# Eight key transposes of one shape, scores in pairs, wider tie matmuls and a hand-written merge at the start of an attention-and-router kernel

## The chip, the cores and the metric

One core of a Trainium2 chip runs the whole kernel. The metric is device time in microseconds (us). Three runs of the kernel before gave 258.41, 258.51 and 258.77; the median is 258.51.

## The reference

```python
# q, k, v: 8 batches x 8 heads x 576 positions x 64
k_p = k.reshape(B, H, Sp, pool, D).mean(axis=3)      # pool = 8, Sp = 72
v_p = v.reshape(B, H, Sp, pool, D).mean(axis=3)
scores = scale * np.matmul(q, k_p.transpose(0, 1, 3, 2))
attn = softmax(scores)
x = (attn @ v_p)            # to 4608 rows x 512
xn = x / (norm(x) + 1e-6);  en = emb / (norm(emb) + 1e-6)
logits = xn @ en.T / tau    # 8 experts
idx = argmax(logits)        # one expert per row
gate_w = softmax(logits)[row, idx]
out[row] = gate_w * (relu(x[row] @ w1[idx]) @ w2[idx])
...
```

Every row goes to one expert. The kernel works on one batch (576 rows) at a time with the expert that most of its rows chose; a loop behind it, empty for these inputs, would handle rows of a batch that chose another.

## The kernel before

The kernel has two kinds of work per batch, and writes their instructions out in one order by hand (a manual schedule): every engine then runs its own instructions in that order. TensorE is written PE in the profile, VectorE DVE, ScalarE ACT, GpSimd POOL, SyncE SP.

The attention side of a batch is a list of steps with costs (`attn_steps`, line 130). `pool_kv` pools keys and values with 18 matmuls of 64-row weights (`pool_mm`, line 140); ScalarE copies the pooled keys to memory in `kp_out` (line 152), VectorE the values in `vp_out`. `qtr` transposes queries, nine per group of four heads (line 191). `kpt` (line 196) transposes the pooled keys of four head pairs into one PSUM tile: per pair one transpose of 128 columns and two of 64 columns with the halves swapped, so that each head's keys exist on partitions 0 to 63 and on 64 to 127. `score` (line 220) makes one head's scores with two matmuls on 64 rows each, and ScalarE takes the exponential (line 237). `pv` (line 241) multiplies by the values for 128 rows, all heads, and VectorE normalises (lines 257, 259). `xtr` (line 264) transposes the result; VectorE copies it (line 275), ScalarE squares it (line 281). `route` (line 284) makes the logits and `count` (line 306) counts the rows per expert; each of the two starts with a matmul of one row that adds a tiny penalty to break ties (lines 287, 307). `expert` (line 313) takes the largest count, and GpSimd reads it into a register and issues the loads of that expert's weights, then of the inputs two batches ahead.

The FFN side (`ffn_steps`, line 422) has eight groups `hgrp` of eight matmuls (line 434), then eight half blocks `yblk` of four matmuls (line 452) and one last step. Results are scaled by the gate and stored on SP's queue.

PSUM has four tiles of two banks, which every one of these steps takes in turn. Weights have three buffers, inputs three, output tiles four.

The order is a merge by due times. Each attention step of batch b has the due time b plus its share of the batch's cost; before an FFN step at position p, all attention steps with due times under p + 1.7 (`LEAD`) are written out. Batch 0's attention is written first as a whole up to its first 128 rows and its expert; the rest of it (its tail) is put among batch 1's steps by due times between 1.0 and 1.4. In batch 0's scores there are extra matmuls on a tile of ones (`fill`, line 214) whose results nobody reads.

Of the kernel before, what the change touches and what calls it, by code (L numbers as in the profile page):

```python
# [11 lines left out]
FP16 = mybir.dt.float16  # L12
# [15 lines left out]
def kernel(  # L28
# [84 lines left out]
    ident_h = const.tile([128, 128], FP16)  # L113
    pmat = const.tile([128, T, G], FP16)
    ones_m = const.tile([128, 512], FP16)
    tie_l = const.tile([1, NC * E], FP16)
    tie_n = const.tile([1, E], FP16)
    half_c = const.tile([128, NC], FP32)
    lnxs = const.tile([128, 1], FP32)
    enT = const.tile([128, 4, E], FP16)  # L120
# [4 lines left out]
    icol = const.tile([128, 1], FP32)  # L125
    pair_b = const.tile([1, B * E], I32)
    pair_e = const.tile([1, B * E], I32)


    def attn_steps(b):  # L130
# [20 lines left out]

        def kp_out(src, h0, nh):

            kp = att.tile([G, nh, 2, D], FP16, name=f"kp{nh}")
            nc.scalar.copy(out=kp, in_=src)
            for hp in range(nh):
                st['kp', h0 + hp] = kp[:, hp]

        def vp_out(src):
            vpx = att.tile([G, HP, 2, D + 1], FP16, name="vpx")  # L160
# [35 lines left out]
        def kpt(h0, nh):  # L196


            pk = psum().bitcast(FP16)
            for hp in range(nh):  # L200
                src = st['kp', h0 + hp]
                nc.tensor.transpose(out=pk[:, ts(2 * hp, G)],
                                    in_=src.rearrange("g r d -> g (r d)"),
                                    identity=ident_h[:G, :G])
                for r in range(2):
                    nc.tensor.transpose(out=pk[ts(r, 64), ts(2 * hp + 1, G)],
                                        in_=src[:, 1 - r], identity=ident_h[:G, :G])
            kpT = att.tile([128, 2 * nh, G], FP16, name=f"kpT{nh}")
            nc.vector.tensor_copy(
                out=kpT, in_=pk[:, 0:2 * nh * G].rearrange("p (h g) -> p h g", g=G))  # L210
            for i in range(2 * nh):
                st['kpT', 2 * h0 + i] = kpT[:, i]

        def fill(cols, n):

            for _ in range(n):
                nc.tensor.matmul(out=cols, lhsT=ones_m[:, 0:128],
                                 rhs=ones_m[:, 0:cols.shape[-1]], start=True, stop=True)

        def score(h, nfill=0):  # L220
            grp, sub, h2 = h // 4, (h // 2) % 2, h % 2
            qT = st['qT', grp]
            pS = psum()
            fill(pS[:, 0:192], nfill)

            for even in (True, False):
                half = sub if even else 1 - sub
                rows = ts(half, 64)
                c0, nb = (512 - 320, 5) if even else (512, 4)
                blk = ds(5 * sub if not even else 4 * sub, nb)  # L230
                nc.tensor.matmul(  # L231
                    out=pS[0:G, c0:c0 + nb * 64].rearrange("g (t p) -> g t p", p=64),
                    lhsT=st['kpT', h if half == 0 else h ^ 1][rows, :],
                    rhs=qT[rows, blk, ts(h2, 64)],
                    start=True, stop=True)
            at = atp.tile([G, S], FP16, name="at")
            nc.scalar.activation(out=at, in_=pS[0:G, 512 - 320:512 + 256], func=AF.Exp,  # L237
                                 scale=escale)
            st['at', h] = at
# [21 lines left out]
                in1=r.unsqueeze(2).to_broadcast([128, H, D]), op=ALU.mult)  # L261
            st['xs'][c] = x_sb

        def xtr(c):
            L = 128 if c < 4 else 64
            x_sb = st['xs'][c]
            xf = x_sb.rearrange("p h d -> p (h d)")
            pt = psum().bitcast(FP16)
            for w in range(4):
                nc.tensor.transpose(out=pt[:, w * 128:w * 128 + L],  # L270
                                    in_=xf[0:L, ts(w, 128)],
                                    identity=ident_h[:L, :L])
            ptv = pt[:, 0:512].rearrange("p (w t) -> p w t", t=128)
            if c < 4:
                nc.vector.tensor_copy(out=xt_all[:, b, :, ts(c, 128)], in_=ptv)  # L275
            else:
                nc.vector.tensor_copy(
                    out=xt_all[:, b, :, ts(c, 128)].rearrange("p w (r t) -> p w r t", r=2),
                    in_=ptv[:, :, 0:L].unsqueeze(2).to_broadcast([128, 4, 2, L]))
            sq = xp.tile([128, H * D], FP16, name="sq", bufs=1)  # L280
            nc.scalar.activation(out=sq, in_=xf, func=AF.Square,  # L281
                                 accum_out=st['ssq'][:, c:c + 1])

        def route(c0, n):

            pl = psum()
            nc.tensor.matmul(out=pl[:, 0:n * E], lhsT=ones_m[0:1, 0:128],
                             rhs=tie_l[:, 0:n * E], start=True, stop=False)
            for c in range(n):
                for w in range(4):  # L290
                    nc.tensor.matmul(out=pl[:, ts(c, E)],
                                     lhsT=xt_all[:, b, w, ts(c0 + c, 128)],
                                     rhs=enT[:, w, :],
                                     start=False, stop=(c == n - 1 and w == 3))
            plv = pl[:, 0:n * E].rearrange("p (c e) -> p c e", e=E)
            if 'lg' not in st:
                st['lg'] = rt.tile([128, NC, E], FP32, name="lg")
                st['lmax'] = rt.tile([128, NC], FP32, name="lmax")
            cs = ds(c0, n)
            lmax = st['lmax'][:, cs]  # L300
            bc = lmax.unsqueeze(2).to_broadcast([128, n, E])
            nc.vector.tensor_reduce(out=lmax, in_=plv, axis=AX.X, op=ALU.max)
            nc.vector.tensor_tensor(out=oh_all[:, b, cs], in0=plv, in1=bc, op=ALU.is_ge)
            nc.vector.tensor_tensor(out=st['lg'][:, cs], in0=plv, in1=bc, op=ALU.subtract)

        def count(cs, pc):
            nc.tensor.matmul(out=pc[:, 0:E], lhsT=ones_m[0:1, 0:128], rhs=tie_n,
                             start=True, stop=False)
            for c in cs:
                nc.tensor.matmul(out=pc[:, 0:E], lhsT=ones_m[:, 0:128],  # L310
                                 rhs=oh_all[:, b, c], start=False, stop=(c == cs[-1]))

        def expert(cs):

            pc = psum()
            count(cs, pc)
            mx = rt.tile([128, E], FP32, name="mx")
            nc.vector.max(out=mx, in_=pc[:, 0:E])
# [26 lines left out]
        if b == 0:  # L345
            for grp in range(2):
# [3 lines left out]
                for h in range(4 * grp, 4 * grp + 4):  # L350
                    step(0.65)(lambda h=h: score(h, (12, 4, 4, 4, 10, 4, 4, 4)[h]))
                    if h == 5:
                        step(1.0)(pool_v)
            step(0.3)(emb_transposed)
            P(0)
            X(0)
            step(0.4)(lambda: route(0, 1))
            step(0.4)(lambda: expert([0]))
            step(0.0)(lambda: load_qkv(2))
            head, steps = steps, []  # L360
            for c in range(1, NC):
                P(c)
                X(c)
            step(0.8)(lambda: route(1, 4))
            step(0.4)(recount)
            return head, steps
# [1 line left out]
        step(0.8)(lambda: qtr(0))  # L368
        step(0.5)(lambda: kpt(0, HP))
        step(0.8)(lambda: qtr(1))  # L370
        for h in range(8):
            step(0.65)(lambda h=h: score(h))
        P(0)
        P(1)
        X(0)
# [132 lines left out]
        return finish  # L508


    def emb_transposed():
        pe = psum().bitcast(FP16)
        for w in range(4):
            nc.tensor.transpose(out=pe[:, ts(w, E)], in_=emb_h[:, ts(w, 128)],
                                identity=ident_h[:E, :E])
        nc.vector.tensor_copy(out=enT, in_=pe[:, 0:4 * E].rearrange("p (w e) -> p w e", e=E))

    with tc.manual_schedule():
# [18 lines left out]
        for i in range(9):  # L537
# [13 lines left out]
                                op=ALU.is_equal)  # L551
        nc.vector.tensor_scalar(out=ident_h, in0=irow, scalar1=icol, scalar2=None,
                                op0=ALU.is_equal)
        nc.vector.tensor_scalar(out=tie_n, in0=irow[0:1, 0:E], scalar1=-2.0 ** -10,
                                scalar2=None, op0=ALU.mult)
        nc.vector.tensor_scalar(
            out=tie_l.rearrange("p (c e) -> p c e", e=E),
            in0=irow[0:1, 0:E].unsqueeze(1).to_broadcast([1, NC, E]),
            scalar1=-2.0 ** -14, scalar2=None, op0=ALU.mult)

# [11 lines left out]
        head, tail = attn_steps(0)  # L572
        for _, f in head:
            f()
        astream = []
        for i, (_, f) in enumerate(tail):
            astream.append((1.0 + 0.4 * i / len(tail), f))
        for b in range(B):
            if b:
                steps = attn_steps(b)  # L580
                total = sum(c for c, _ in steps)
                done = 0.0
                for c, f in steps:
                    astream.append((b + done / total, f))
                    done += c
            for i, f in enumerate(gate_steps(b)):
                astream.append((b + LEAD + 0.05 + 0.12 * i, f))
        astream.sort(key=lambda s: s[0])
        j = 0
        for b in range(B):  # L590
            steps = ffn_steps(lambda b=b: xt_all[:, b], lambda b=b: weights[b],
# [1 line left out]
            total = sum(c for c, _ in steps)  # L593
            done = 0.0
            for c, f in steps:
                while j < len(astream) and astream[j][0] < b + done / total + LEAD:
                    astream[j][1]()
                    j += 1
                f()
# [80 lines left out]
```

## Time and profile before

| what | value |
|---|---|
| median of three runs | 258.51 us |
| the profiled execution | 257.43 us |
| its span, first to last instruction | 255.8 us |
| TensorE busy | 90% |
| TensorE weight loads (overlap) | 56% |
| VectorE, ScalarE, GpSimd busy | 51%, 42%, 17% |
| mean granted TensorE clock | 0.954 of full |
| DMA, software queue; hardware queue | 70.1%; 12.5% of 16 engines |

The busy time of TensorE counts a matmul from its first column to its modelled end, and neighbours overlap, so distances from start to start say more than durations. The granted clock is 1.00 at 2.4 GHz and 0.50 at 1.2 GHz. A DMA share can be over 1, since packets on one engine overlap.

### The profile page before, as it was taken

The page shows a single profiled execution, that of the slowest core. Times are in us where ns is not written, and L with a number is a line of the kernel's source. Part 1 is how long each engine was busy: PE and PEld are TensorE (multiplying, and loading weights), DVE is VectorE, ACT ScalarE, POOL GpSimd, SP SyncE. Part 2 cuts the span into 40 slices and gives each one's busy share as a digit, 9 for nine tenths or more (in the row PEclk, how much of TensorE's full clock was granted, in tenths as well). Part 3 has the DMA queues.
Part 4 walks back from the last instruction along what each step waited for, and adds up shares of the span by engine and source line. Part 5 has one row for each costly group of instructions (what it writes and reads, how often), then busy time and mean ns, then how long its engine had stood idle before and what let it go on. Part 6 is the DMA issues. An engine that isn't in the chain of part 4 may idle for free. (4 is left out here: it accounts for less than half of the span.)

```text
span 255.8 us, 5655 instructions
## 1 busy us (share of the span) xinstructions
PE 230.0 (90%) x2272; PEld 143.2 (56%) x2273; DVE 129.5 (51%) x368; ACT 108.1 (42%) x221; POOL 42.9 (17%) x61
## 2 busy tenths in 40 slices
PE   7796788999989998999899998999899999996950
PEld 3574555764566546673676456654666377564520
DVE  3225564862576428661685257642876178414310
ACT  3342364524463355417362446335541746124120
POOL 7300510060003400070006100340004000400000
PEclk9998755999999999999999999999999999999995
DMA  5994899249993999589994999299968952597061
GB/s 76 194 208 81 145 209 208 50 75 210 212 257 51 202 200 247 140 139 211 230 215 65 213 209 258 53 204 201 243 146 135 209 118 55 93 208 215 3 145 46
DMA packets 27597, 40.79 MB, mean 159 GB/s; under 512 B 1960, under 2 KB 15272, under 8 KB 27568
## 3 DMA queue, kind: packets, MB, share of 16 engines
q0 software_dynamic: 21152, 30.94, 70.1%
q1 hardware_dynamic: 6416, 9.46, 12.5%
q8 instruction: 19, 0.31, 0.5%
q14 instruction: 10, 0.08, 0.1%
HBM read 61.88 MB, written 9.44 MB: 279 GB/s over the span
## 5 line engine op out<-in xcount | busy, mean ns | idle before, releaser
L434 PE MATMUL pa<-xt_all,w 128*128 128x288 f16 x512 | 71.9, 288 | 2.4 <-ACT y_sb L482 2.4
L452 PE MATMUL pa<-w,hT 128*128 128x512 f16 x256 | 63.7, 380 | 0.0
L434 PEld LDWEIGHTS <-w 128*128 128x128 f16 x512 | 47.3, 99 | 16.5 <-issue 5.0
L237 ACT ACTIVATE at<-pa 72x576 f16<-72x576 f32 x64 | 38.2, 642 | 34.1 <-PE pa L231 33.9
L452 PEld LDWEIGHTS <-hT 128*128 128x128 f16 x256 | 21.5, 97 | 23.9 <-issue 2.8
L93 POOL DMA_DIRECT2D w<-in_moe_w_dram x8 | 6.3, 791 | 169.8 <-DVE vpx L161 145.7
L441 ACT ACTIVATE hT<-pa 128x576 f16<-128x576 f32 x32 | 20.7, 650 | 29.3 <-PE pa L434 29.1
L464 DVE TENSOR_SCALAR y_sb<-pa,gm 128x512 f32<-128x512 f32 x16 | 12.0, 751 | 34.9 <-PE pa L452 34.9
L259 DVE TENSOR_TENSOR x_sb<-pa,r 128x512 f16<-128x512 f32 x40 | 27.7, 691 | 2.6
L281 ACT ACTIVATE sq<-x_sb 128x512 f16<-128x512 f16 x40 | 25.0, 625 | 7.1 <-DVE x_sb L259 6.7
L443 DVE TENSOR_SCALAR hT<-pa 128x576 f16<-128x576 f32 x32 | 24.1, 753 | 5.5 <-PE pa L434 5.3
L462 ACT ACTIVATE y_sb<-pa,gm 128x512 f32<-128x512 f32 x16 | 11.0, 687 | 37.2 <-DVE y_sb L464 37.2
L250 PE MATMUL pa<-vpx,at 72*128 72x65 f16 (+1 forms) x384 | 19.7, 201 | 2.7 <-ACT hT L441 1.1
L250 PEld LDWEIGHTS <-at 72*128 72x128 f16 (+1 forms) x384 | 16.5, 106 | 9.8 <-issue 3.7
L270 PE MATMUL pa<-ident_h,x_sb 128*128 128x128 f16 (+1 forms) x160 | 15.2, 223 | 6.8 <-DVE x_sb L259 3.8
L145 PE MATMUL pa<-kv,pmat 64*72 64x512 f16 (+2 forms) x180 | 19.5, 366 | 0.0
L231 PE MATMUL pa<-qT,kpT 64*72 64x256 f16 (+1 forms) x128 | 18.8, 320 | 0.5
L257 DVE RECIPROCAL r<-pa 128x8 f32<-128x8 f32 x40 | 8.1, 202 | 22.1 <-PE pa L250 22.0
L270 PEld LDWEIGHTS <-x_sb 128*128 128x128 f16 (+1 forms) x160 | 10.6, 100 | 13.0 <-issue 5.4
L193 DVE COPY qT<-pa 128x1152 f16<-128x1152 f16 x16 | 12.1, 757 | 11.1 <-PE pa L191 10.2
L231 PEld LDWEIGHTS <-kpT 64*72 64x72 f16 x128 | 6.5, 111 | 16.0 <-issue 13.3
L275 DVE COPY xt_all<-pa 128x512 f16<-128x512 f16 x32 | 13.3, 415 | 2.2 <-PE pa L270 2.0
(94 smaller groups left out, 202.8 us busy)
## 6 DMA issues: line engine op xcount, KB each, us to landing
w<-in_moe_w_dram POOLq DMA_DIRECT2D x16, 1024.0 KB, 10.5
out_dram<-y_sb SPq DMA_DIRECT2D x64, 128.0 KB, 6.2
kv<-in_v_dram POOLq DMA_DIRECT2D x8, 576.0 KB, 19.0
kv<-in_k_dram POOLq DMA_DIRECT2D x7, 576.0 KB, 15.2
qq<-in_q_dram POOLq DMA_DIRECT2D x7, 576.0 KB, 22.9
out_dram<-y_sb SPq DMA_DIRECT2D x16, 64.0 KB, 5.8
kv<-in_k_dram POOLq DMA_DIRECT2D x2, 288.0 KB, 5.3
qq<-in_q_dram POOLq DMA_DIRECT2D x2, 288.0 KB, 6.3
```

Of the source, the lines that this page charges most:

```text
L145: nc.tensor.matmul(out=pk[0:G, par * 512 + c0:par * 512 + c0 + na * nh * D], lhsT=pmat[rows, t, :], rhs=kv[rows, a0:a0 + na, h0:h0 + nh, t ...
L231: nc.tensor.matmul(out=pS[0:G, c0:c0 + nb * 64].rearrange("g (t p) -> g t p", p=64), lhsT=st['kpT', h if half == 0 else h ^ 1][rows, :], r ...
L237: nc.scalar.activation(out=at, in_=pS[0:G, 512 - 320:512 + 256], func=AF.Exp, scale=escale)
L250: nc.tensor.matmul(out=px[rows, h * 128:h * 128 + D + 1], lhsT=st['at', h][:, c * 128:c * 128 + L], rhs=st['vpx'][:, h // 2, h % 2, :], st ...
L259: nc.vector.tensor_tensor(out=x_sb, in0=pxv[:, :, 0:D], in1=r.unsqueeze(2).to_broadcast([128, H, D]), op=ALU.mult)
L270: nc.tensor.transpose(out=pt[:, w * 128:w * 128 + L], in_=xf[0:L, ts(w, 128)], identity=ident_h[:L, :L])
L275: nc.vector.tensor_copy(out=xt_all[:, b, :, ts(c, 128)], in_=ptv)
L281: nc.scalar.activation(out=sq, in_=xf, func=AF.Square, accum_out=st['ssq'][:, c:c + 1])
L434: nc.tensor.matmul(out=ph[:, half * 512:half * 512 + HALF], lhsT=w1v[:, kk, w // 2, w % 2, :], rhs=xt()[:, kk, ts(half, HALF)], start=(kk ...
L441: nc.scalar.activation(out=dst, in_=src, func=AF.Relu)
L443: nc.vector.tensor_scalar(out=dst, in0=src, scalar1=0.0, scalar2=None, op0=ALU.max)
L452: nc.tensor.matmul(out=py, lhsT=st['hT'][:, w // 2, w % 2, ts(c, 128)], rhs=w2[:, w // 2, w % 2, :], start=(w == 0), stop=(w == 7))
```

## The change

Key transposes: the key tile gets nine heads' room for eight heads (2 x nh + 1), and a second ScalarE copy puts head 0 behind the last one. Eight transposes each take the 128 columns of two neighbouring heads, every next one 64 columns further; head i is then on partitions 0 to 63 of slot i and on 64 to 127 of slot i - 1.

Scores: batches 1 to 7 have steps of two heads with twice the cost.

Tie matmuls: the two penalty tiles get 128 rows, of which all but the first are zero, and the matmuls use all rows.

Start: fills are added ahead of the embedding transposes (8), and in batch 0's first transpose (14), route (8) and expert (12); batch 0's tail interleaves products and transposes, and 18 steps of it and of batch 1's first eight are written in a fixed order. The lead is 1.5 at the first FFN step and rises to 1.7 at the end of batch 0's FFN. The gate steps have a list of their own, sorted in with the rest.

```diff
-    tie_l = const.tile([1, NC * E], FP16)
-    tie_n = const.tile([1, E], FP16)
+    tie_l = const.tile([128, NC * E], FP16)
+    tie_n = const.tile([128, E], FP16)
...
-            kp = att.tile([G, nh, 2, D], FP16, name=f"kp{nh}")
-            nc.scalar.copy(out=kp, in_=src)
-            for hp in range(nh):
-                st['kp', h0 + hp] = kp[:, hp]
+            kp = att.tile([G, 2 * nh + 1, D], FP16, name=f"kp{nh}")
+            nc.scalar.copy(
+                out=kp[:, 0:2 * nh].rearrange("g (h r) d -> g h r d", r=2), in_=src)
+            nc.scalar.copy(out=kp[:, 2 * nh], in_=src[:, 0, 0])
+            st['kp', h0] = kp
...
-            for hp in range(nh):
-                src = st['kp', h0 + hp]
-                nc.tensor.transpose(out=pk[:, ts(2 * hp, G)],
-                                    in_=src.rearrange("g r d -> g (r d)"),
+            src = st['kp', h0].rearrange("g h d -> g (h d)")
+            for i in range(2 * nh):
+                nc.tensor.transpose(out=pk[:, ts(i, G)], in_=src[:, i * D:i * D + 128],
                                     identity=ident_h[:G, :G])
-                for r in range(2):
-                    nc.tensor.transpose(out=pk[ts(r, 64), ts(2 * hp + 1, G)],
-                                        in_=src[:, 1 - r], identity=ident_h[:G, :G])
...
-        def xtr(c):
+        def xtr(c, nfill=0):
...
-            pt = psum().bitcast(FP16)
+            pt = psum()
+            fill(pt[:, 512:704], nfill)
+            pt = pt.bitcast(FP16)
...
-            nc.tensor.matmul(out=pl[:, 0:n * E], lhsT=ones_m[0:1, 0:128],
+            fill(pl[:, 512:704], nfill)
+            nc.tensor.matmul(out=pl[:, 0:n * E], lhsT=ones_m[:, 0:128],
                              rhs=tie_l[:, 0:n * E], start=True, stop=False)
...
-            nc.tensor.matmul(out=pc[:, 0:E], lhsT=ones_m[0:1, 0:128], rhs=tie_n,
+            nc.tensor.matmul(out=pc[:, 0:E], lhsT=ones_m[:, 0:128], rhs=tie_n,
                              start=True, stop=False)
...
-            step(0.3)(emb_transposed)
+            step(0.3)(lambda: emb_transposed(8))
             P(0)
-            X(0)
-            step(0.4)(lambda: route(0, 1))
-            step(0.4)(lambda: expert([0]))
+            step(0.6)(lambda: xtr(0, 14))
+            step(0.4)(lambda: route(0, 1, 8))
+            step(0.4)(lambda: expert([0], 12))
...
-            for c in range(1, NC):
-                P(c)
-                X(c)
+            P(1)
+            P(2)
+            X(1)
+            P(3)
+            X(2)
+            P(4)
+            X(3)
+            X(4)
...
-        for h in range(8):
-            step(0.65)(lambda h=h: score(h))
+        for h in range(0, 8, 2):
+            step(1.3)(lambda h=h: [score(h), score(h + 1)])
...
+                for f in [s1[0], tail[0], s1[1], tail[1], tail[2], s1[2], s1[3], tail[3],
+                          tail[4], s1[4], tail[5], tail[6], s1[5], tail[7], s1[6], tail[8],
+                          s1[7], tail[9]]:
+                    f()
+                astream = astream[8:]
...
+        def lead(pos):
+            return pos + LEAD - 0.2 * max(0.0, 1.0 - pos)
...
-                while j < len(astream) and astream[j][0] < b + done / total + LEAD:
+                while j < len(astream) and astream[j][0] < lead(b + done / total):
```

## Rows read from the trace of the kernel before

**Rows 1.** Busy time by stretch, one period of the steady state; columns in the first line.
```profile
core 0: us, PE busy (x) PEld busy (x) DVE busy (x) ACT busy (x) POOL busy (x), PEclk, DMA share, GB/s
...
79.10:106.70 27.60, 26.73 (x275) 16.54 (x273) 15.65 (x43) 13.12 (x28) 4.98 (x6) 1.00 0.96 185
```

**Rows 2.** Busy time by stretch, the start; columns as above.
```profile
19.40:23.10 3.70, 1.68 (x24) 1.20 (x23) 1.88 (x7) 1.47 (x4) 0.00 (x0) 1.00 0.75 129
...
24.00:27.00 3.00, 3.00 (x16) 1.09 (x12) 0.73 (x2) 0.00 (x0) 1.75 (x3) 0.50 0.06 8
...
28.00:30.00 2.00, 0.61 (x12) 0.44 (x8) 1.97 (x5) 0.64 (x3) 0.98 (x2) 1.00 1.09 197
...
31.00:44.00 13.00, 10.98 (x120) 7.44 (x120) 7.59 (x20) 7.51 (x16) 1.20 (x1) 0.50 1.16 209
```

**Rows 3.** Timeline of TensorE at the start: start us, us, engine, line, operation, count.
```profile
9.27 1.16 PE L217 MATMUL pa<-ones_m 128*128 128x192 f16 x12
...
23.48 3.69 PE L145 MATMUL pa<-kv,pmat 64*72 64x512 f16 x18
...
40.16 0.68 PE L250 MATMUL pa<-vpx,at 72*128 72x65 f16 x9 [0.30 <-ACT at L237]
...
42.81 1.91 PE L434 MATMUL pa<-xt_all,w 128*128 128x288 f16 x8
```

**Rows 4.** Timeline of TensorE, key transposes of a steady batch.
```profile
83.62 1.14 PE L434 MATMUL pa<-xt_all,w 128*128 128x288 f16 x8
84.60 0.20 PE L202 MATMUL pa<-ident_h,kp 72*128 72x72 f16 x1
84.73 0.22 PE L206 MATMUL pa<-ident_h,kp 72*64 72x72 f16 x2
...
85.76 0.68 PE L191 MATMUL pa<-ident_h,qq 128*128 128x128 f16 x9
```

**Rows 5.** Timeline of TensorE, scores and values products between FFN blocks.
```profile
87.23 0.46 PE L231 MATMUL pa<-qT,kpT 64*72 64x320 f16 x4
87.62 1.04 PE L452 MATMUL pa<-w,hT 128*128 128x512 f16 x4
88.59 0.32 PE L231 MATMUL pa<-qT,kpT 64*72 64x320 f16 x2
88.84 1.04 PE L452 MATMUL pa<-w,hT 128*128 128x512 f16 x4
...
92.37 0.71 PE L231 MATMUL pa<-qT,kpT 64*72 64x320 f16 x4
93.01 1.04 PE L452 MATMUL pa<-w,hT 128*128 128x512 f16 x4
...
94.43 1.03 PE L452 MATMUL pa<-w,hT 128*128 128x512 f16 x4
95.30 0.42 PE L250 MATMUL pa<-vpx,at 72*128 72x65 f16 x8
95.56 1.03 PE L452 MATMUL pa<-w,hT 128*128 128x512 f16 x4
```

**Rows 6.** Groups of ScalarE from 25 to 40 us: busy us, mean ns, idle before.
```profile
L237 ACT ACTIVATE at<-pa 72x576 f16<-72x576 f32 x8 | 4.7, 644 | 1.1 <-PE pa L231 1.1
L281 ACT ACTIVATE sq<-x_sb 128x512 f16<-128x512 f16 x4 | 2.5, 630 | 3.8 <-DVE x_sb L259 3.8
...
L155 ACT CAST kp<-pa 72x512 f16<-72x512 f32 x1 | 0.6, 581 | 5.0 <-PE pa L145 5.0
```

**Rows 7.** Timeline of TensorE, count with its tie matmul, and merged pooling.
```profile
77.69 1.14 PE L434 MATMUL pa<-xt_all,w 128*128 128x288 f16 x8
78.76 0.17 PE L307 MATMUL pa<-tie_n,ones_m 1*128 1x8 f16 x1
78.87 0.28 PE L310 MATMUL pa<-oh_all,ones_m 128*128 128x8 f16 x5
79.08 2.13 PE L145 MATMUL pa<-kv,pmat 64*72 64x512 f16 x18
```

More of the change, by code (lines that the diff above doesn't have):

```diff
@@ L127, with fill @@
     pair_e = const.tile([1, B * E], I32)
+    def fill(cols, n):
+        for _ in range(n):
+            nc.tensor.matmul(out=cols, lhsT=ones_m[:, 0:128],
+                             rhs=ones_m[:, 0:cols.shape[-1]], start=True, stop=True)
     def attn_steps(b):
@@ L211, in kpt @@
             for i in range(2 * nh):
[L212 to L218, printed above, removed]
+                st['kpT', 2 * h0 + i, 0] = kpT[0:64, i]
+                st['kpT', 2 * h0 + (i + 1) % (2 * nh), 1] = kpT[64:128, i]
         def score(h, nfill=0):
@@ L232, in score @@
                     out=pS[0:G, c0:c0 + nb * 64].rearrange("g (t p) -> g t p", p=64),
-                    lhsT=st['kpT', h if half == 0 else h ^ 1][rows, :],
+                    lhsT=st['kpT', h, half],
                     rhs=qT[rows, blk, ts(h2, 64)],
@@ L282, in xtr, with route @@
                                  accum_out=st['ssq'][:, c:c + 1])
-        def route(c0, n):
+        def route(c0, n, nfill=0):
             pl = psum()
-            nc.tensor.matmul(out=pl[:, 0:n * E], lhsT=ones_m[0:1, 0:128],
+            fill(pl[:, 512:704], nfill)
+            nc.tensor.matmul(out=pl[:, 0:n * E], lhsT=ones_m[:, 0:128],
                              rhs=tie_l[:, 0:n * E], start=True, stop=False)
@@ L311, in count, with expert @@
                                  rhs=oh_all[:, b, c], start=False, stop=(c == cs[-1]))
-        def expert(cs):
+        def expert(cs, nfill=0):
             pc = psum()
+            fill(pc[:, 512:704], nfill)
             count(cs, pc)
@@ L508, in store, with emb_transposed @@
         return finish
-    def emb_transposed():
-        pe = psum().bitcast(FP16)
+    def emb_transposed(nfill):
+        pe = psum()
+        fill(pe[:, 512:704], nfill)
+        pe = pe.bitcast(FP16)
         for w in range(4):
@@ L553 @@
                                 op0=ALU.is_equal)
-        nc.vector.tensor_scalar(out=tie_n, in0=irow[0:1, 0:E], scalar1=-2.0 ** -10,
+        nc.vector.memset(tie_n, 0.0)
+        nc.vector.memset(tie_l, 0.0)
+        nc.vector.tensor_scalar(out=tie_n[0:1], in0=irow[0:1, 0:E], scalar1=-2.0 ** -10,
                                 scalar2=None, op0=ALU.mult)
         nc.vector.tensor_scalar(
-            out=tie_l.rearrange("p (c e) -> p c e", e=E),
+            out=tie_l[0:1].rearrange("p (c e) -> p c e", e=E),
             in0=irow[0:1, 0:E].unsqueeze(1).to_broadcast([1, NC, E]),
@@ L574 @@
             f()
-        astream = []
-        for i, (_, f) in enumerate(tail):
-            astream.append((1.0 + 0.4 * i / len(tail), f))
+        astream, gstream = [], []
+        tail = [f for _, f in tail]
         for b in range(B):
@@ L585 @@
                     done += c
+            if b == 1:
+                s1 = [f for _, f in astream]
+                for f in [s1[0], tail[0], s1[1], tail[1], tail[2], s1[2], s1[3], tail[3],
[3 more added lines that the diff above has]
+                astream = astream[8:]
             for i, f in enumerate(gate_steps(b)):
-                astream.append((b + LEAD + 0.05 + 0.12 * i, f))
-        astream.sort(key=lambda s: s[0])
+                gstream.append((b + LEAD + 0.05 + 0.12 * i, f))
+        astream = sorted(astream + gstream, key=lambda s: s[0])
+        def lead(pos):
+            return pos + LEAD - 0.2 * max(0.0, 1.0 - pos)
         j = 0
```

## The prediction

> **What bounds the kernel now.** I read the views in this order: the busy table of the page, the stretches by window, the timeline of TensorE, the waits. The page has TensorE busy 90% of the span and no other engine above 56%; the chain of waits names only the last microseconds, so it does not help. Cut into batches, the picture is sharper: one period from a merged pooling (keys and values) to the next is 27.6 us, TensorE is busy 26.73 us of it, VectorE 15.65, ScalarE 13.12, at full clock, and the DMA share is 0.96 where 13 us of loads hold 1.16 [rows 1, 2]. So from batch 2 on TensorE's instruction order is the time: a microsecond taken out of its queue is a microsecond, as long as the consumers keep up. The start is another regime: the clock falls to half (1.2 GHz) from 24 to 27 us and again from 31 to 44 us, and TensorE waits there for VectorE and ScalarE [rows 2, 3].
>
> **Part 1, key transposes (lines 196 to 212).** Before, the four head pairs of a batch take four full transposes (72x128) and eight half ones (72x64). They run from 84.60 to 85.76, 1.16 us for 12 instructions; each change between the two shapes costs about 0.13 (84.60 to 84.73 for one transpose) [rows 4]. After, 8 equal 72x128 transposes. The trace has no stream of just these; the nearest is the values product, 72x128 weights with 65 columns: 8 in 95.30 to 95.56 = 0.26, 0.033 each [rows 5]. With 72 columns 0.036, so 0.29. Saved: 0.87 per batch. Bounds: nine query transposes take 0.68 with their tail, 0.075 each at most [rows 4], so 0.60 for eight, saved 0.56; at 72 columns in 2.4 GHz cycles, 0.030 each, 0.92 saved. I take 0.87, since shape and columns are almost those of the row.
> The price is a second ScalarE copy (72x64) behind the key copy, and VectorE's value copy waits for ScalarE there. The key copy of 72x512 takes 0.58 [rows 6], so the new one lies between 0 and 0.58; I estimate 0.2 by its eighth of the columns plus a fixed part. In the steady state three FFN groups and a query transpose lie between pooling and the key transposes (the order in the code), which hides it; without that cover it is 6 x 0.2 = 1.2. I charge 0.4 in all (0 to 1.2).
>
> **Part 2, scores in pairs.** Worked out from the costs and due times in the code, the eight scores of a batch stand in five visits between FFN blocks (2, 1, 2, 1, 2) and will stand in four of two. A visit of two takes 0.39 (87.23 to 87.62), of one 0.25 (88.59 to 88.84), the last of two 0.64 (92.37 to 93.01), and the FFN block ahead of a visit is longer by 0.10: four FFN matmuls take 0.97 before a visit (87.62 to 88.59) and 0.87 before a values product (94.43 to 95.30) [rows 5]. The visits at 89.81 and 91.15 repeat the first two. Before: 0.39 + 0.25 + 0.39 + 0.25 + 0.64 + 5 x 0.10 = 2.42. After: 4 x (0.39 + 0.10) = 1.96. Saved 0.46; if the 0.25 excess of the last visit (by its place a wait for a free buffer) stays, 0.21. Score 7 is issued earlier than before against the first values product, so what is late next there is not ScalarE.
>
> **Part 3, tie matmuls of 128 rows.** The one-row matmul changes the array's shape twice: the 8 FFN matmuls ahead of it take 1.07 (77.69 to 78.76) against 0.98 with a 128-row successor (83.62 to 84.60), and it holds the queue 0.11 itself (78.76 to 78.87) [rows 4, 7]. The routing one at 77.06 repeats this. After, each is one more small product of the kind behind it, about 0.03. Saved per batch 2 x (0.09 + 0.11 - 0.03) = 0.34; bounds 0.25 to 0.40. The larger tie tiles cost two memsets at the start, behind loads that TensorE waits for anyway: nothing.
>
> **Sum of the steady state.** 0.87 + 0.46 + 0.34 = 1.67 for each of batches 2 to 7, 10.0 us; batch 1's route and count add 0.34: 10.4. Low 6 x (0.56 + 0.21 + 0.25) + 0.25 = 6.4; high 6 x (0.92 + 0.46 + 0.40) + 0.40 = 11.1. TensorE's own idle time, about 0.9 of 27.6, stays as it is in this sum. The DMA share of 0.96 becomes about 1.02 by the shorter period, still under 1.16; the weights are issued where the expert is known, over half an FFN ahead, and that distance shrinks by about 1.2 us.
>
> **Part 4, the start: fills.** From 19.4 to 23.1 TensorE was busy 1.68 of 3.7 us, and at 24 the clock was half [rows 2]. The 42 new fill matmuls are under 0.097 each (12 in 1.16 [rows 3]), about 3.5 us in all, so they fill that hole. The cheaper key transposes of batch 0 (two halves, about 0.4 each, less the extra copies) bring the stretch forward by about 0.6, and the fills overrun their waits by about that much (an estimate: 12 of them, over 0.9, stand ahead of the last wait, which is for three short VectorE steps): the expert's decision and the first weight issue on GpSimd's queue stay where they are. So merged pooling of batch 1 starts at about 23.3 and runs at full clock, 2.13 us as at 79.08 [rows 7], instead of 3.69 [rows 3]: it ends at 25.4, 1.7 us earlier.
>
> **Part 5, the merge of batch 0's tail with batch 1.** In the new written order the pooling goes first and eight scores follow in four pairs. ScalarE must do, from 25.4 on, the key copies 0.8, four squares 2.5 and eight exponentials 4.7 [rows 6]: 8.0 us, so the last exponential is not done before 33.4. Before, the way from the end of pooling (23.48 + 3.69 = 27.2) to that point was 13.0 us (the values product of batch 1 waits for it until 40.16 [rows 3]); as slow as that it would be 38.4. I take 38.0, near the slow end: right behind the pooling VectorE is busy 1.97 of 2 us while TensorE waits [rows 2], the value copy, the query copies, the normalisations and the x copies all pass through it one by one, and in the new order the last four exponentials still come behind the last x copy. The new lead puts only the first values product of batch 1 ahead of the first FFN group, so that starts at about 38.3 instead of 42.81 [rows 3], with four steps left over (two values products, two transposes) that cost about 0.26 each between FFN steps, as the values product at 95.30 [rows 5]: 1.0. Gain 42.8 - 39.3 = 3.5. From 26.5 to 38 TensorE has less to do per microsecond than in 31 to 44, where 10.98 busy of 13 us, at half rate, left it at half clock, and in 28 to 30 it was busy 0.61 of 2 us just before the fall [rows 2]; so I expect the half clock until about 3 us after the first FFN group, which costs 1.5 there where before it cost 0.8. Net 2.8. Bounds: 8 with the first FFN group at 34, -1 with the half clock kept through its first ten microseconds.
> Batch 1's expert comes two FFN groups later in the order; its weights have a whole FFN to land, and the stores on SP's queue keep their places.
>
> **Total.** 10.4 - 0.4 + 2.8 = 12.8. The profiled execution is 257.43 (span 255.8 and 1.63 around it): 244.6. The median of the runs is 1.08 higher, so I predict 245.7.
>
> A rule that speaks against part 1: the eight values products above have weights on all 72 rows and yet follow each other at 0.033 [rows 5]. The Trainium skill (TensorE: Matmul & The Clock Gate, Part 3: Packing small matmuls) says that a weight load runs beside a matmul in flight only where the two use different row groups. By that rule the new transposes, all on the same rows, would not overlap, and part 1 would shrink as in the third rival; the row disagrees with it.
>
> **Rivals.**
> 1. The clock stays full through the start. For it: the fills show a way, and pooling is long. Against it: 28 to 30 [rows 2]. The first FFN group then starts at about 37, no half clock after it: 2.6 more, 243.1.
> 2. The start gives nothing: as many waits as before, half clock until deep in FFN 0, head at -1. For it: 13 us at half clock now [rows 2] with the same steps. 3.8 less: 249.5. If only the fills fail and pooling still runs at half clock, 1.6 less: 247.3.
> 3. The eight transposes do not overlap, at 0.13 each as the isolated one (84.60 to 84.73 [rows 4]): 1.04, saved 0.12 instead of 0.87; 6 x 0.75 = 4.5 less, 250.2.
> 4. Slower: pairs of scores starve for PSUM. There are four buffers; the FFN output holds one, a pair takes two. If each pair waits for an exponential (0.64 [rows 6]) of the pair before, 28 pairs cost 18 us: 264. It decides the sign from 12.8/28 = 0.46 us per pair. For it: the last visit already takes 0.64 where the first takes 0.39 [rows 5]. Against it: FFN blocks of 0.87 separate the pairs, and pairs ran at 87.23 without such a wait.
> 5. The shape changes cost the same in the new order (the change does not do what it says): nothing but four transposes less per batch, 7 x 4 x 0.036 = 1.0: 257.5.
>
> **How the numbers follow.** My forecast 0.58 (own range 242 to 248), rival 1 0.12, rival 2 0.19 with its smaller form, rival 3 0.04, rival 4 0.04, rival 5 0.03. For 8 in 10 the range reaches to rivals 1 and 3: 241.5 to 250.5. A measurement of this kernel can tell about 0.2% (0.5 us) from no change: faster 0.94, same 0.02, slower 0.04.
>
> **What would show it.** In the profile after: a period of about 26.0 us; eight equal transposes in about 0.3; four score visits of under 0.4 each; no gap before the tie matmuls; the merged pooling of batch 1 in about 2.1 us; the first FFN group near 38. Wrong if the period stays above 27, if a pair of scores stands 0.6 or more, if the half clock lasts beyond 42, or if VectorE or ScalarE ends TensorE's waits in the middle.

## The result, and the profile after

The changed kernel takes 246.43 us (median of 4 runs, 246.23 to 246.61) against 258.64 for the kernel before in the same series: a ratio of 0.951, 95% interval 0.945 to 0.957. The forecast was 245.7 with a range of 241.5 to 250.5. The profiled execution is 246.23, 11.2 less than that of before. Medians here and below are of all executions, but ratios only of those within 1.5% of the fastest of their kernel, so a ratio need not be the quotient of two medians.

From the page of the changed kernel: the span, the busy table and the granted clock in 40 slices (tenths).

```profile
span 244.6 us, 5695 instructions
...
PE 218.2 (89%) x2282; PEld 140.7 (58%) x2283; DVE 128.1 (52%) x370; ACT 108.9 (45%) x230; POOL 42.9 (18%) x61
...
PEclk9999957999999999999999999999999999999995
```

TensorE lost about as much busy time (230.0 to 218.2) as the span lost, so its share hardly moved (90% and 89%). The half clock is now shorter. By stretch, changed kernel (columns as in [rows 1]; the column before the last two is the clock):

```profile
19.40:23.10 3.70, 3.70 (x55) 3.51 (x55) 1.97 (x8) 0.72 (x2) 0.00 (x0) 1.00 0.64 109
...
28.00:30.00 2.00, 1.82 (x24) 1.21 (x23) 1.97 (x5) 0.85 (x4) 0.71 (x1) 0.88 1.12 202
...
31.00:36.00 5.00, 4.50 (x65) 2.75 (x61) 2.64 (x10) 4.52 (x11) 1.20 (x1) 0.50 1.12 212
...
38.00:40.00 2.00, 2.00 (x17) 1.45 (x16) 0.83 (x2) 1.26 (x3) 0.00 (x0) 0.56 1.23 208
40.00:42.00 2.00, 2.00 (x30) 1.72 (x29) 1.49 (x5) 0.06 (x1) 0.00 (x0) 1.00 1.21 207
...
101.50:127.90 26.40, 25.11 (x272) 16.02 (x268) 15.51 (x43) 13.28 (x29) 4.97 (x6) 1.00 0.98 191
```

The hole of 19.4 to 23.1 is filled, the fall of the clock at 24 [rows 2] is gone, the second fall comes at 29.5 and ends before 40 instead of at 44. The last row is one steady period: 26.4 us where [rows 1] has 27.6.

TensorE's timeline of the changed kernel, the lines that answer to [rows 3], [rows 7], [rows 4] and [rows 5] in turn, and one that answers to none (the first two lines, fills and a score of batch 0, are used in the last section):

```profile
8.48 1.16 PE L132 MATMUL pa<-ones_m 128*128 128x192 f16 x12
9.58 0.32 PE L230 MATMUL pa<-qT,kpT 64*72 64x320 f16 x2
...
22.89 2.13 PE L151 MATMUL pa<-kv,pmat 64*72 64x512 f16 x18
24.95 0.43 PE L249 MATMUL pa<-vpx,at 72*128 72x65 f16 x8
...
36.48 2.11 PE L442 MATMUL pa<-xt_all,w 128*128 128x288 f16 x8
...
72.45 1.14 PE L442 MATMUL pa<-xt_all,w 128*128 128x288 f16 x8
73.43 0.17 PE L309 MATMUL pa<-tie_n,ones_m 128*128 128x8 f16 x1
73.46 0.27 PE L312 MATMUL pa<-oh_all,ones_m 128*128 128x8 f16 x5
74.40 2.13 PE L151 MATMUL pa<-kv,pmat 64*72 64x512 f16 x18 [0.68 <-DMA kv<-in_v_dram]
...
79.92 0.42 PE L210 MATMUL pa<-ident_h,kp 72*128 72x72 f16 x8
80.18 0.67 PE L199 MATMUL pa<-ident_h,qq 128*128 128x128 f16 x9
...
81.65 0.46 PE L230 MATMUL pa<-qT,kpT 64*72 64x320 f16 x4
82.04 1.04 PE L460 MATMUL pa<-w,hT 128*128 128x512 f16 x4
...
95.31 0.38 PE L271 MATMUL pa<-ident_h,x_sb 128*128 128x128 f16 x4 [1.64 <-DVE xt_all L276]
```

Merged pooling takes 2.06 (22.89 to 24.95), the first FFN group stands at 36.48, the tie matmul holds the queue 0.03 and the FFN group ahead of it is back at 0.98, eight transposes take 0.26 (79.92 to 80.18), a pair of scores 0.39. The last line is new in its size: 1.64 us in which TensorE waits for an x copy.

Where the 11.2 us are can be read from the places of the last FFN step, the first and the sixth of them (two lines before, two after):

```profile
69.23 1.06 PE L474 MATMUL pa<-w,hT 128*64 128x256 f16 x16
...
207.95 1.06 PE L474 MATMUL pa<-w,hT 128*64 128x256 f16 x16
```

```profile
63.97 1.06 PE L482 MATMUL pa<-w,hT 128*64 128x256 f16 x16
...
197.11 1.06 PE L482 MATMUL pa<-w,hT 128*64 128x256 f16 x16
```

The first of these stands at 69.23 before and 63.97 after, 5.26 earlier. The sixth stands at 207.95 and 197.11: 5.58 more in five periods, 1.12 per batch. The rest, 0.36, lies behind. The steady state was forecast at 1.67 per batch.

What TensorE waited for from 46 us on, changed kernel (us in total, times, longest):

```profile
PE pa L271 <- DVE xt_all L276: 4.9, 5, 1.6
PE pa L442 <- ACT y_sb L490: 2.5, 1, 2.5
PE pa L249 <- ACT hT L449: 1.1, 5, 0.2
PE pa L249 <- ACT at L236: 0.9, 5, 0.2
PE pa L151 <- DMA kv<-in_v_dram: 0.7, 1, 0.7
```

In the kernel before the same first line is smaller:

```profile
PE pa L270 <- DVE xt_all L275: 2.9, 5, 0.7
```

VectorE's timeline of the changed kernel around the wait of 1.64 names the cause:

```profile
85.83 0.75 DVE L472 TENSOR_SCALAR y_sb<-pa,gm 128x512 f32<-128x512 f32 x1 [3.92 <-PE pa L460]
...
94.45 0.48 DVE L488 TENSOR_SCALAR y_sb<-pa,gm 64x256 f32<-64x256 f32 x1 [1.87 <-DMA out_dram<-y_sb]
94.85 0.41 DVE L276 COPY xt_all<-pa 128x512 f16<-128x512 f16 x1
```

An FFN writes five output tiles and there are four buffers. The fifth (94.45) takes the buffer of the first, written at 85.83 and still being stored; VectorE waits 1.87 us for that store, and the x copy that TensorE needs is queued behind. The shorter queue brings the fifth tile closer to the first, and the store does not get shorter. Of the five waits of this kind the profile puts two down to the store by name; that the others are the same is shown by the runs with five tiles below.

### The profile page after: what moved, and what is told of

It is laid out like the page before. It is cut to its first block, busy times and chain, and to the rows that moved or that the text cites. A ratio compares the mean times of both kernels' runs of the same rounds, so it can differ in the third digit from the quotient of the medians.

```text
span 244.6 us, 5695 instructions
## 1 busy us (share of the span) xinstructions
PE 218.2 (89%) x2282; PEld 140.7 (58%) x2283; DVE 128.1 (52%) x370; ACT 108.9 (45%) x230; POOL 42.9 (18%) x61
## 5 line engine op out<-in xcount | busy, mean ns | idle before, releaser
L442 PE MATMUL pa<-xt_all,w 128*128 128x288 f16 x512 | 72.7, 290 | 2.6 <-ACT y_sb L490 2.5
L460 PE MATMUL pa<-w,hT 128*128 128x512 f16 x256 | 62.9, 380 | 0.0
L249 PE MATMUL pa<-vpx,at 72*128 72x65 f16 (+1 forms) x384 | 19.2, 199 | 2.9 <-ACT at L236 1.2
L271 PE MATMUL pa<-ident_h,x_sb 128*128 128x128 f16 (+1 forms) x160 | 14.7, 217 | 6.8 <-DVE xt_all L276 4.9
L151 PE MATMUL pa<-kv,pmat 64*72 64x512 f16 (+2 forms) x180 | 17.5, 336 | 0.7 <-DMA kv<-in_v_dram 0.7
L230 PE MATMUL pa<-qT,kpT 64*72 64x320 f16 (+1 forms) x128 | 17.0, 316 | 0.7 <-ACT at L236 0.2
L230 PEld LDWEIGHTS <-kpT 64*72 64x72 f16 x128 | 5.7, 112 | 12.8 <-issue 9.8
## 6 DMA issues: line engine op xcount, KB each, us to landing
kv<-in_v_dram POOLq DMA_DIRECT2D x8, 576.0 KB, 19.4
```

The source lines that it names most:

```text
L151: nc.tensor.matmul(out=pk[0:G, par * 512 + c0:par * 512 + c0 + na * nh * D], lhsT=pmat[rows, t, :], rhs=kv[rows, a0:a0 + na, h0:h0 + nh, t ...
L230: nc.tensor.matmul(out=pS[0:G, c0:c0 + nb * 64].rearrange("g (t p) -> g t p", p=64), lhsT=st['kpT', h, half], rhs=qT[rows, blk, ts(h2, 64) ...
L249: nc.tensor.matmul(out=px[rows, h * 128:h * 128 + D + 1], lhsT=st['at', h][:, c * 128:c * 128 + L], rhs=st['vpx'][:, h // 2, h % 2, :], st ...
L271: nc.tensor.transpose(out=pt[:, w * 128:w * 128 + L], in_=xf[0:L, ts(w, 128)], identity=ident_h[:L, :L])
L442: nc.tensor.matmul(out=ph[:, half * 512:half * 512 + HALF], lhsT=w1v[:, kk, w // 2, w % 2, :], rhs=xt()[:, kk, ts(half, HALF)], start=(kk ...
L460: nc.tensor.matmul(out=py, lhsT=st['hT'][:, w // 2, w % 2, ts(c, 128)], rhs=w2[:, w // 2, w % 2, :], start=(w == 0), stop=(w == 7))
```

## The experiments

Totals of one kernel spread by up to 6 us within a run here, and the two profiled executions of the changed kernel are already 3.2 us apart at batch 1's pooling, so the readings rest on stretches of the profiled executions: the period is a quarter of the way from the third to the seventh merged pooling. Before it is 27.74, changed 26.52; run again beside others, 26.36. Two more runs below, without fills and with the old merge, leave the steady state as changed and have 26.91 and 26.62: with four output tiles the period of one order of instructions differs by 0.5 between executions, with five tiles, in two runs, by 0.01.

**The changed kernel again.** No edit; the reference on the second chip.

> The changed kernel itself, as the reference for the runs beside it, because the start (the first loads) and the last weight load differ by some microseconds from chip to chip. Theory: 0.951 of the kernel before (0.945 to 0.957). Rival: with a later start on this chip the gain of the first 40 us goes, 0.965. In the trace four periods from the third to the seventh merged pooling should take 106.1 us, with TensorE waiting about 0.6 to 1.6 us per batch for the x copy.

Measured: 248.97, ratio 0.950 (0.938 to 0.962). Merged pooling of batch 1 starts at 26.10 instead of 22.89. The ratio holds; the rival falls.

**Old key transposes in the changed kernel.** The edit, shortened:

```diff
-            for i in range(2 * nh):
-                nc.tensor.transpose(out=pk[:, ts(i, G)], in_=src[:, i * D:i * D + 128], ...)
+            for hp in range(nh):        # and one key copy, as before
+                nc.tensor.transpose(...)          # 72x128
+                for r in range(2):
+                    nc.tensor.transpose(...)      # 72x64
```

> The changed kernel (246.4) with the old key transposes and the single key copy. Theory: each pair of shape changes in the array costs about 0.29 and eight equal transposes cost 0.26, so undoing costs 0.90 in each of batches 1 to 7 and about 0.5 in batch 0, less what the second copy cost (0 to 1): 252.5 (251.5 to 253.5). Rival: only the four instructions less per batch count, at 0.036 each: 247.5. Second rival: the second copy behind the key copy takes back most of it: 249.

Measured: 254.41, ratio 0.977 (0.968 to 0.986). Its pooling of batch 1 starts at 27.48, so the total says little; the period is 27.39 (79.51 to 189.08), 0.5 to 1.0 over the four with the changed steady state. The two rivals (0.15 and 0.4 per batch) fall by that, the second narrowly; the fine value comes with five tiles below.

**Single scores in batches 2 to 7.**

```diff
-        for h in range(0, 8, 2):
-            step(1.3)(lambda h=h: [score(h), score(h + 1)])
+        for h in range(8):              # b >= 2; batch 1 keeps pairs
+            step(0.65)(lambda h=h: score(h))
```

> The changed kernel with single scores in batches 2 to 7. Theory: a fifth visit costs 0.46 of TensorE per batch, but a later wait, in which the last FFN output tile waits for the store of the first, shrinks by what the visits behind the first output take (about 0.4 in four of six batches), so the total is 247 to 247.8. Rival: the whole 0.46 comes back in six batches: 249.2. Second rival: the pairs cost as much as they save, 246.4.

Measured: 249.24, ratio 0.960 (0.953 to 0.967), with the pooling of batch 1 at 25.68. The period is 26.13 (76.92 to 181.43): shorter than with pairs (26.36 to 26.91), although the queue has one visit more. Its waits for the x copy are 1.4 us in all instead of 4.0 to 6.0. So with four buffers the pairs cost more than they save; I had expected them to come out a little ahead.

**One-row tie matmuls.**

```diff
-    lhsT=ones_m[:, 0:128], rhs=tie_n,
+    lhsT=ones_m[0:1, 0:128], rhs=tie_n[0:1],      # and the same in route
```

> The changed kernel with the one-row tie matmuls. Theory: each costs two shape changes, 0.18 more, 18 of them of which 16 stand in dense stretches: 249.3 (248.8 to 249.7). Rival: one-row matmuls are no dearer and the earlier gap is something else: 246.4.

Measured: 250.69, ratio 0.958 (0.949 to 0.967); the period is 26.66 (77.52 to 184.14), within the 26.36 to 26.91 of the changed steady state, so the period alone shows no cost. TensorE's timeline does:

```profile
102.69 1.14 PE L442 MATMUL pa<-xt_all,w 128*128 128x288 f16 x8
103.76 0.17 PE L309 MATMUL pa<-tie_n,ones_m 1*128 1x8 f16 x1
103.87 0.28 PE L312 MATMUL pa<-oh_all,ones_m 128*128 128x8 f16 x5
```

The FFN group ahead takes 1.07 again instead of 0.98, and the tie matmul holds the queue 0.11 instead of 0.03: 0.17, where the theory has 0.18. The rival (none) falls.

**No new fills.** The four calls, shortened:

```diff
-    emb_transposed(8), xtr(0, 14), route(0, 1, 8), expert([0], 12)
+    emb_transposed(0), xtr(0, 0), route(0, 1, 0), expert([0], 0)
```

> The changed kernel without the 42 new fills at the start (32 matmuls of batch 0's scores stay). Theory: TensorE is idle from 19 to 22, the clock falls before the merged pooling, which takes 3.6 instead of 2.1, the decision on the expert comes 0.3 earlier, the rest of the merge is bound by VectorE and ScalarE as before: 247.5 (247 to 248). Rival: the full clock through the pooling also carries the merge, without it the merge runs slower throughout: 249 or more. Second rival: the fills hold nothing, 246.0.

Measured: 252.17, ratio 0.963 (0.950 to 0.975). TensorE's timeline without fills:

```profile
20.42 0.25 PE L524 MATMUL pa<-ident_h,emb_h 8*128 8x8 f16 x4
...
24.42 4.06 PE L151 MATMUL pa<-kv,pmat 64*72 64x512 f16 x18
28.41 0.62 PE L249 MATMUL pa<-vpx,at 72*128 72x65 f16 x8
```

The pooling takes 3.99 (24.42 to 28.41) at half clock; but from the end of the scores to the pooling are 4.00 us, with fills 4.55. From the end of the scores to the first last FFN step it takes 46.39 (20.42 to 66.81), with fills 45.63 (18.34 to 63.97). In the second execution of the changed kernel it takes 46.01 (21.55 to 67.56). So the fills are worth 0.4 to 0.8, below the theory's 1.1; that they are worth more than nothing is not shown beyond the 0.4 by which two executions of one kernel differ. The total is as high as the first rival has it, but the steady state, which the fills do not touch, has a share in that (a period of 26.91), and the merge behind the pooling is not slower: from the end of the pooling to the first last FFN step it takes 38.40 (28.41 to 66.81), with fills 39.02 (24.95 to 63.97).

**The old order of the merge.** The edit, shortened:

```diff
-    P(1), P(2), X(1), P(3), X(2), P(4), X(3), X(4)
+    P(1), X(1), P(2), X(2), ...                 # merged by due times 1.0 to 1.4
-    return pos + LEAD - 0.2 * max(0.0, 1.0 - pos)
+    return pos + LEAD
```

> The changed kernel with the old order of batch 0's tail (by due times, product and transpose alternating) and the old lead of 1.7 throughout; fills, transposes, pairs and ties as changed. Theory: the fills carry the pooling (1.6 us) and the order the rest of the start (2 us): 2 to 3 us slower than the changed kernel beside it. Rival: the gain of the start is the clock and the shorter transposes alone, no more than 0.7 slower. Second rival: all 3.7 us of the start are lost, 250.

Measured: 248.8, ratio 0.961 (0.953 to 0.968) beside 0.950, with intervals that overlap. From the start of the pooling to the first last FFN step it takes 42.61 (24.64 to 67.25); the changed kernel 41.08 and 41.46. So the order and the lead are worth 1.2 to 1.5, by one execution against two: less than the theory's 2 and twice the first rival's 0.7; the second rival falls.

**Five output tiles, changed kernel.** The loop that never runs takes its tile from the same buffers, which makes the room.

```diff
-    yp = ctx.enter_context(tc.tile_pool(name="yp", bufs=4))
+    yp = ctx.enter_context(tc.tile_pool(name="yp", bufs=5))
-                o_sb = yp.tile([128, DM], FP32, name="o_sb", bufs=1)
+                o_sb = yp.tile([128, DM], FP32, name="y_sb")
```

> The changed kernel with five output tiles instead of four (the loop that never runs shares them). Theory: TensorE's waits for the x copy (4.9 us in five batches) and the 2.5 us wait in the last FFN come from the fifth output tile of an FFN, whose buffer is held by the store of the first one; VectorE waits there and all behind it is late. With five tiles both go: 6 to 7 us less than the changed kernel beside it, four periods in 103.3. Rival: VectorE is late by its own load, then at most 1 us is won. Second rival: the transfers themselves are the bound and the wait moves to the next load: 2 to 3 us.

Measured: 239.52, ratio 0.924 (0.917 to 0.930), beside 0.950 for the changed kernel on that chip: the fastest version here; the last one below is level with it. The period is 25.22, from the third to the seventh merged pooling:

```profile
75.39 2.13 PE L151 MATMUL pa<-kv,pmat 64*72 64x512 f16 x18 [1.37 <-DMA kv<-in_v_dram]
...
176.25 2.13 PE L151 MATMUL pa<-kv,pmat 64*72 64x512 f16 x18
```

TensorE's waits from 46 us on, the first two:

```profile
PE pa L151 <- DMA kv<-in_v_dram: 1.4, 1, 1.4
PE pa L249 <- ACT at L236: 0.9, 5, 0.2
...
```

The line of the x copy and that of the last FFN are gone, as the theory says; both rivals fall. The four periods took 100.9 us where the theory had 103.3: the store had cost more than the two lines of waits show, and the wait of the values product for `hT` (0.2 per batch) is gone with them. The wait for values of batch 3 grew from 0.7 to 1.4, once in the run.

**Five output tiles, kernel before.** The same edit.

> The kernel before with five output tiles. Theory: its own smaller waits of that kind (2.9 us for the x copy, 2.4 in the last FFN) go: 4.5 to 5.3 less than before, a ratio of 0.980. Rival: no gain, 1.000, if the store was not the holder. The difference of this and the changed kernel with five tiles should then be 13 to 14 us, more than the 12.2 of the change, if pairing and shorter transposes had run into the store.

Measured: median 253.85 (249.75 to 254.62) beside 259.9; there is no interval for its ratio. The period is 26.89, 0.86 less than 27.74:

```profile
80.59 2.13 PE L145 MATMUL pa<-kv,pmat 64*72 64x512 f16 x18
...
188.13 2.13 PE L145 MATMUL pa<-kv,pmat 64*72 64x512 f16 x18
```

TensorE waits for nothing from 46 us on that the profile shows. Five tiles give the kernel before 0.86 per batch and the changed one 1.1 to 1.3; the difference of the two periods is 1.67, the number forecast for the steady state.

**Five tiles and single scores.** Both edits above.

> The changed kernel with five output tiles and single scores in batches 2 to 7. With four tiles single scores were faster over four periods (104.5 us against 106.1 and 105.5 with pairs). Theory: a pair saves 0.46 per batch in TensorE's queue, and four tiles took it back through the store; with five tiles singles should cost 0.46 per batch: a period of 25.67 instead of 25.21, total 242.2. Rival: pairs are no gain of themselves, then 25.2 or less, total 239.5 or less.

Measured: 241.69, ratio 0.929 (0.921 to 0.936); period 25.59 (76.28 to 178.65), 0.38 over pairs. With room for the store the pairs are a gain, a little under 0.46.

**Five tiles and twelve equal transposes.**

```diff
-            for i in range(2 * nh):
+            for i in list(range(2 * nh)) + list(range(nh)):
```

> The changed kernel with five output tiles and twelve key transposes per batch, all of 72x128 (the first four are written twice), as many as before the change. Theory: the shape changes were the price, the number is not: 4 x 0.033 = 0.13 per batch, a period of 25.35, total 240.3. Rival: the number of transposes was the price: 0.30 to 0.45 per batch, a period of 25.5 to 25.7, 241.5 to 242.5.

Measured: 242.21, ratio 0.932 (0.925 to 0.939), with a late start (pooling at 26.92 instead of 24.44). The period is 25.35 (77.47 to 178.86), 0.13 more, as the theory has it. TensorE's timeline:

```profile
82.99 0.56 PE L210 MATMUL pa<-ident_h,kp 72*128 72x72 f16 x12
83.38 0.67 PE L199 MATMUL pa<-ident_h,qq 128*128 128x128 f16 x9
```

**Five tiles and the old transposes.** The edit of the first experiment.

> The changed kernel with five output tiles and the old key transposes (four of 72x128, eight of 72x64, single copy). Theory: 0.90 per batch, a period of 26.1 instead of 25.21, total 245.5 to 246. Rival: in four tiles the cost over four periods was 0.8 per batch; if part of it was the store, 0.6 or less and a period under 25.8.

Measured: 244.3, ratio 0.939 (0.931 to 0.947); period 26.12 (76.86 to 181.35), 0.91 more. TensorE's timeline:

```profile
82.38 0.20 PE L209 MATMUL pa<-ident_h,kp 72*128 72x72 f16 x1
82.51 0.22 PE L213 MATMUL pa<-ident_h,kp 72*64 72x72 f16 x2
82.67 0.21 PE L209 MATMUL pa<-ident_h,kp 72*128 72x72 f16 x1
...
83.54 0.68 PE L198 MATMUL pa<-ident_h,qq 128*128 128x128 f16 x9
```

Twelve instructions in both: 0.39 when all have one shape, 1.16 when two shapes alternate. The shape changes were the price, not the number. A half transpose also writes the other half of the output partitions, but that is not what costs: the two of a pair take 0.22 each and both lie within the 0.22 from 82.51, side by side. The time goes where the width changes, 0.13 on the way from the full to the half and 0.16 back.

**Five tiles and more fills.** The edit, shortened:

```diff
+            XF = lambda c, n: step(0.6)(lambda: xtr(c, n))
-            X(1) ... X(2) ... X(3) X(4)
+            XF(1, 14) ... XF(2, 4) ... XF(3, 6) XF(4, 6)
+            nf = 4 if b == 1 else 0
-            step(1.3)(lambda h=h: [score(h), score(h + 1)])
+            step(1.3)(lambda h=h, nf=nf: [score(h, nf), score(h + 1, nf)])
```

> The changed kernel with five output tiles and fills also in the merge: 14, 4, 6, 6 in the four transposes of batch 0's tail and 4 in each score of batch 1. Theory: the merge is bound by VectorE and ScalarE, so fills cost nothing there, and they keep the clock full until the FFN is dense; the 6 to 10 us of half clock around the first FFN groups go, 2 us less: 237.5. Rival: the fills lie on the path (each waits for the same buffers as the work behind it) and cost 1 to 2 us, the clock gains as much: 239.5. Second rival: the clock falls all the same and the fills run at half rate: 241.

Measured: 239.9, ratio 0.923 (0.917 to 0.929), the same as without. The stretch 36 to 41 us, first with more fills, then with five tiles alone:

```profile
36.00:41.00 5.00, 4.74 (x67) 3.06 (x68) 1.06 (x5) 4.07 (x8) 1.20 (x1) 1.00 1.14 211
```

```profile
36.00:41.00 5.00, 4.65 (x38) 3.15 (x37) 1.95 (x5) 2.52 (x6) 0.39 (x1) 0.50 1.15 209
```

The clock stays full to the end, and the first FFN group starts 15.7 us after the pooling (25.33 to 41.02) instead of 12.9 (24.44 to 37.37), 2.8 later; from there to the first last FFN step it takes 25.9 instead of 28.0, 2.1 less. The fills are on the path and take what the clock gives: the first rival.

## Why the prediction was right

**Key transposes.** Forecast 0.29 for eight and 0.87 saved; measured 0.26, and 0.91 per batch by undoing it with five tiles. The twelve equal ones at 0.033 each show that the row of the values products was the right neighbour. The third rival (0.13 each) is refuted by that row. So is, for these transposes, the rule that the prediction cites from the Trainium skill (TensorE: Matmul & The Clock Gate, Part 3: Packing small matmuls), as it is worded there: all twelve have weights on the same 72 rows, their weight loads take 0.10 each, and yet they follow each other at 0.033.

**Second key copy.** Charged with 0.4 in all. The 0.91 of the undoing is net of it and as large as the saving in TensorE's own queue (1.16 - 0.26 = 0.90), so where three FFN groups cover it, it costs nothing that shows.

**Scores.** Visits and lengths came as forecast (four, 0.39 each in the steady batches). The worth with five tiles is 0.38: the last pair now stands so close to the first values product that this waits 0.19 for an exponential, where I had written that ScalarE would not be late there. The fourth rival, waits of a pair for PSUM, showed only in batch 2, 0.43 us in all by two waits.

**Ties.** Forecast 0.34. The gap is gone (73.43, 73.46); by the difference of the five-tile kernels what is left for the ties is 1.67 - 0.91 - 0.38 = 0.38. The timeline with one-row ties has 0.17 for the one of `count`; twice that, for two per batch, is 0.34.

**The step that failed** is a sentence of the sum: that TensorE's own idle time "stays as it is". The queue became 1.67 shorter per batch (shown with five tiles) but the period only 1.12 to 1.38, since the wait for the store of the first output tile grew: 2.9 to 4.9 us in five batches. That is 2.0 of the 2.8 us missing from five periods; the wait of 0.7 for values of batch 3 is nearly all the rest. I had asked of each engine whether it would keep up, and of the weights; the output tiles I had left out, though the kernel before waited there already. One of the prediction's signs of being wrong came with it: VectorE ends TensorE's waits in the middle, and the period is 26.4 to 26.5 instead of about 26.0.

The runs with four tiles say the same when the wait for the x copy is taken off. In the four periods it is 2.3 us before, and 4.1, 3.5, 5.7 and 4.5 in the four executions with the changed steady state (the changed kernel twice, without fills, old merge). A quarter of it off the period leaves 27.17 before and 25.49, 25.49, 25.49 and 25.50: 1.67 less. With old transposes, single scores and one-row ties (4.0, 1.1 and 3.1) it leaves 26.39, 25.85 and 25.88, which is 0.90, 0.36 and 0.39 more.

**The start** made up for part of it. Up to the first last FFN step 5.26 us were won; of that my sum had 0.87 + 0.46 + 0.34 for batch 1's ties and batch 2's work and 2.8 for the start, 4.47. The pooling ran at full clock, 2.06, ending at 24.95 against 25.4 forecast; the first FFN group came at 36.48 against 38.3; the half clock came as expected and ended about where it was said (forecast: until 3 us after that group; measured: 3.3). The error is the length of the merge, 11.5 us (24.95 to 36.48) instead of 12.9: I had put it near the old 13.0. The first rival's full clock was not there; enforced by fills, with five tiles, it was worth nothing.

Sum: 0.8 more at the start, 2.8 less in five periods, 0.4 charged for the key copy and not paid: 1.6 less than the 12.8 forecast for the profiled execution. The medians of forecast and result differ by 0.7. That the total came so near is in part luck: the steady state gave 2.8 less than the sum had, and two errors the other way, at the start and at the key copy, covered 1.2 of it.

## What to carry to other kernels

In a dense TensorE queue count the changes of shape, not the instructions: small matmuls of one shape ran at 0.03 us each here, and a detour to fewer columns (the half transposes) or to one row (the ties) cost about 0.1 us on the way in and as much on the way out. When a queue gets shorter, look at every buffer that a store or load gives back: its time does not shrink, and a buffer that was nearly late becomes the bound. A wait in one engine's queue is paid by the work behind it; here one missing output buffer cost 1.1 to 1.3 us per batch, about as much as the change won there.

## What the runs showed of the hardware

The clock recorded as granted does not show the first half-rate stretch. In the repeated run of the changed kernel, fills of 192 columns at 9.65 take 0.17 each, twice the 0.09 of the first run (8.48 to 9.58 in its timeline above), while the record says full clock; from the query transposes ahead of them to the second pooling takes 7.42 us there (8.46 to 15.88) and 4.82 in the first run (7.84 to 12.66), which is 2.6 of the 3.2 us between the two executions:

```profile
9.65 2.12 PE L132 MATMUL pa<-ones_m 128*128 128x192 f16 x12
11.69 0.48 PE L230 MATMUL pa<-qT,kpT 64*72 64x320 f16 x2
```

And the store of one output tile, 256 KB on SP's queue, can hold its buffer for 7.9 us (86.6, the end of the first output tile's scaling, to 94.45) while loads hold the DMA engines (a share of 1.16 in that stretch).

Two transposes of 64 columns into different halves of the output partitions run side by side (two of 0.22 within 0.22), while going from 128 columns to 64 and back takes 0.13 and 0.16.
